# Polynomial-sketch attention into a tanh FFN: VectorE's attention written as one numbered sequence, q loaded and laid out by load, groups cut at batch 0's end

## The chip, the cores and the metric

The kernel runs on one core of a Trainium2 chip. The engines are TensorE (PE in the rows, its weight loads PEld), VectorE (DVE), ScalarE (ACT), GpSimd (POOL) and SyncE (SP), which here only issues transfers. Each engine works through its own list of instructions in order. The metric is the device time of one execution in microseconds, and less is better.

## The reference

```python
batch, n_heads, seq, head_dim = 4, 4, 1088, 32          # r = 8, d_model 128, d_ff 2048
a, b = S1 @ x, S2 @ x                                   # 8 numbers each, for every row x of q and of k
phi(x) = outer(a, b).reshape(64)
kv  = einsum('bhsf,bhsd->bhfd', phi(k), v);   z = phi(k).sum(over s)
attn = (phi(q) @ kv) / (phi(q) @ z + 1e-6)              # [4, 4, 1088, 32]
x = attn.transpose(0, 2, 1, 3).reshape(4352, 128)
h = x @ w_in;   out = (h - tanh(h)) @ w_out             # 4352 x 2048 between
```

## The kernel before, in words

**Attention of a batch.** k and q of a batch (four heads, 1088 rows) lie in 34 chunks of 32 columns and are turned by VectorE (`kT<-kL` L485, `qT<-qL` L559). TensorE makes the sketches of k (L491), which VectorE turns back (`abk<-psa`, L496). VectorE forms the outer products `w` in three pieces (L522), and TensorE sums them with v (L532). A small product `gram`, `gm`, `sc` (L505 to L515) gives the denominators. `kvd` and `kvb` bring the sum into place. The q side does the same: sketch (L570), `abq` (L575), `cq` (L586), then `m`, `den`, `rd`, `ap` (the division, L598 to L607), the outer products `qp` (L623), their transposition `qpT` (L628), and 32 products with `kvb` on TensorE (L636), each kept as two in the trace. ScalarE or VectorE copies the result into `xT`, bf16, 128 x 4352 columns. Everything of the attention on TensorE goes into four PSUM banks, `psa`. The q side works on blocks of 128 columns: batch 0 in the pieces 0 to 2, 2 to 5 and 5 to 9, the other batches in 0 to 5 and 5 to 9.

**FFN.** The columns of `xT` are cut into groups (`GCOLS`). For each group 16 products with slices of w_in (L699, "first products") go to three PSUM banks `psh`; ScalarE takes tanh of each (`th`, L702); 16 products with w_out (L712) and two with the folded weight w_in·w_out (`wch`, `wcl`, L716) add up in one bank `pso`. VectorE turns the sum (`ot`, L721), and four or eight transfers write it out. So 34 products of TensorE and 16 tanh of ScalarE go with each group. The folded weight is made at the start from casts of the weights (`wi`, `wo`), transposes (`wiT`) and 16 small products.

**What sets the order.** A planner in the program (`_Prog.schedule`) holds estimated durations, takes for each engine the operation that can start first, and among those that can start within 30 ns of it the one with the smallest key; the result is one fixed list per engine. Keys are due times: the attention of batch b is due some microseconds ahead of the group that needs it. When TensorE has nothing for over 350 ns before the first group, it gets filler products on zeros (L367). SyncE's queue issues the loads in the order of their keys.

Of the kernel before, what the change touches and what calls it, by code (L numbers as in the profile page):

```python
# [816 lines left out]
```

## Time and profile before

| | us |
|---|---|
| time, median of three runs | 131.1 (130.19 to 131.17) |
| the profiled execution, its own time | 132.3 |
| its span, first to last instruction | 130.5 |
| busy: TensorE / ScalarE / VectorE / GpSimd | 111.9 / 85.2 / 72.1 / 1.8 |

The span is what the trace covers; 1.8 us of the profiled execution lie outside it. Busy times overlap between engines and are means over stages that differ.

### The profile page before, as it was taken

Reading aid. Unit: us, or ns where it says so; the run is one execution under the profiler, and the core shown is the slowest. Engines: PE = TensorE matmul, PEld = TensorE weight load, DVE = VectorE, ACT = ScalarE, POOL = GpSimd, SP = SyncE. Lnnn points to the kernel's source line nnn. Section 1 sums busy time; section 2 is a strip of 40 time slices with the busy share of each in tenths; the row PEclk is TensorE's granted clock in tenths of the full one; section 3 lists DMA queues with packets and bytes.
Section 4 is the critical chain, followed back from the end, with each engine's and each line's share of the span. In section 5 each row is a group of like instructions: output and inputs, shape, how many; then the busy total and the mean of one; then the engine's idle time right before and its main releaser. Section 6 shows DMA issues by size and latency. Waiting matters only on the chain.

```text
span 130.5 us, 3757 instructions
## 1 busy us (share of the span) xinstructions
PE 111.9 (86%) x1602; PEld 54.7 (42%) x1618; DVE 72.1 (55%) x155; ACT 85.2 (65%) x189; POOL 1.8 (1%) x14
## 2 busy tenths in 40 slices
PE   6998989674048899899899999999999999999990
PEld 4856656341022452333543444453335433334460
DVE  5368678496934969963728982641997201002010
ACT  0315822751014269578587899659789999999990
POOL 4100000000000000000000000000000000000000
PEclk9999999999855699999999999999999999999999
DMA  2999999999700000040000410400040130401322
GB/s 43 287 312 343 337 222 319 209 306 201 166 20 0 0 8 0 5 68 17 0 0 5 65 15 18 68 5 0 0 71 14 28 57 0 70 10 25 61 39 41
DMA packets 25552, 11.28 MB, mean 86 GB/s; under 512 B 19136, under 2 KB 24000, under 8 KB 25536
## 3 DMA queue, kind: packets, MB, share of 16 engines
q1 hardware_dynamic: 24528, 10.44, 35.4%
q10 hardware_dynamic: 1008, 0.61, 1.8%
q8 instruction: 12, 0.20, 0.7%
q14 instruction: 4, 0.03, 0.1%
HBM read 8.81 MB, written 2.23 MB: 85 GB/s over the span
## 4 chain that ended last, share of the span: by engine, by line
PE 48%; SPq 12%; DVE 12%; ACT 11%; DMA 11%; issue 3%
PE pso L712 16%; PE psh L699 16%; SPq L393 12%; DMA qL<-in_q_dram 11%; ACT th L702 10%; PE psa L636 6%; PE psa L532 3%; DVE w L522 3%; PE pso L716 2%; PE psa L491 2%; DVE abk L496 2%; DVE ot L721 1%; DVE qT L559 1%; PE psa L570 1%; ACT xT L318 1%
## 5 line engine op out<-in xcount | busy, mean ns | idle before, releaser
L702 ACT ACTIVATE th<-psh 128x512 bf16<-128x512 f32 (+3 forms) x160 | 72.0, 566 | 10.2 <-PE psh L699 9.3
L699 PE MATMUL psh<-xT,wi 128*128 128x512 bf16 (+3 forms) x152 | 51.9, 353 | 2.7 <-ACT th L702 1.2
L712 PE MATMUL pso<-th,wo 128*128 128x512 bf16 (+3 forms) x154 | 49.3, 349 | 1.1 <-issue 0.5
L699 PEld LDWEIGHTS psh<-xT,wi 128*128 128x128 bf16 x160 | 15.3, 98 | 24.2 <-ACT th L702 14.7
L712 PEld LDWEIGHTS pso<-th,wo 128*128 128x128 bf16 x160 | 15.3, 98 | 19.2 <-ACT th L702 7.0
L721 DVE STREAM_TRANSPOSE ot<-pso 128x512 f32<-128x512 f32 (+3 forms) x10 | 6.3, 635 | 25.7 <-PE pso L712 25.7
L636 PE MATMUL psa<-qpT,kvb 32*32 32x128 f32 (+3 forms) x576 | 10.1, 294 | 6.8 <-DVE qpT L628 6.8
L318 ACT CAST xT<-psa 128x384 bf16<-128x384 f32 (+3 forms) x11 | 5.1, 479 | 14.5 <-PE psa L636 14.5
L367 PE MATMUL pso<-zz 128*128 128x256 bf16 x86 | 12.6, 296 | 1.1 <-DVE zz L366 1.1
L628 DVE STREAM_TRANSPOSE qpT<-qp 128x512 f32<-128x512 f32 (+1 forms) x16 | 11.5, 755 | 0.1
L623 DVE TENSOR_TENSOR qp<-ap,abq 128x512 f32<-128x512 f32 (+1 forms) x16 | 11.3, 744 | 0.2
L522 DVE TENSOR_TENSOR w<-abk 128x768 f32<-128x768 f32 x12 | 11.1, 949 | 0.1
L636 PEld LDWEIGHTS psa<-qpT,kvb 32*32 32x32 f32 x576 | 6.6, 106 | 10.4 <-DVE qpT L628 7.5
L367 PEld LDWEIGHTS pso<-zz 128*128 128x128 bf16 x86 | 8.6, 106 | 3.2 <-DVE zz L366 1.1
L496 DVE STREAM_TRANSPOSE abk<-psa 128x288 f32<-128x288 f32 x8 | 3.4, 459 | 8.1 <-PE psa L491 8.1
L559 DVE STREAM_TRANSPOSE qT<-qL 128x448 f32<-128x448 f32 (+3 forms) x9 | 6.1, 673 | 2.9 <-DMA qL<-in_q_dram 2.9
L532 PE MATMUL psa<-w,vL 128*32 128x64 f32 x288 | 6.5, 223 | 1.2 <-DVE w L522 1.2
L575 DVE STREAM_TRANSPOSE abq<-psa 128x288 f32<-128x288 f32 (+3 forms) x12 | 3.9, 359 | 6.3 <-PE psa L570 6.3
L485 DVE STREAM_TRANSPOSE kT<-kL 128x576 f32<-128x576 f32 (+1 forms) x8 | 5.6, 718 | 3.1 <-DMA kL<-in_k_dram 3.1
L532 PEld LDWEIGHTS psa<-w,vL 128*32 128x32 f32 x288 | 4.7, 110 | 4.2 <-DVE w L522 3.6
L662 ACT CAST wi<-wi_f 128x512 bf16<-128x512 f32 x4 | 2.5, 620 | 4.5 <-DMA wi_f<-in_moe_w_in_dram 4.3
L491 PE MATMUL psa<-kT,wab 64*32 64x288 f32 x64 | 3.4, 481 | 1.3 <-ACT xT L318 1.1
(54 smaller groups left out, 59.1 us busy)
## 6 DMA issues: line engine op xcount, KB each, us to landing
kL<-in_k_dram SPq DMA_DIRECT2D x3, 544.0 KB, 11.9
vL<-in_v_dram SPq DMA_DIRECT2D x9, 144.0 KB, 12.5
wi_f<-in_moe_w_in_dram SPq DMA_DIRECT2D x4, 256.0 KB, 6.2
wo_f<-in_moe_w_out_dram SPq DMA_DIRECT2D x4, 256.0 KB, 7.2
out_dram<-ot SPq DMA_DIRECT2D x16, 64.0 KB, 2.0
qL<-in_q_dram SPq DMA_DIRECT2D x3, 320.0 KB, 13.8
qL<-in_q_dram SPq DMA_DIRECT2D x4, 224.0 KB, 12.7
vL<-in_v_dram ACTq DMA_DIRECT2D x3, 144.0 KB, 3.9
```

What stands on the lines that cost most here:

```text
L367: filler = (lambda e, n: e.matmul(bank_o.slots[0][0][:, 0:256], zz.ap[:, 0:128], zz.ap[:, 128:384], start=True, stop=True), zop, bank_o)
L393: return P.add({eng: (430.0, 0.0)}, lambda e, n: e.dma_start(out=o_, in_=i_), w=w, key=key, dma=nbytes)
L522: P.add(_v(768), lambda e, n, p=p, wv=wv: e.tensor_tensor(out=wv.ap.rearrange("p (x i j) -> p x i j", i=8, j=8), in0=abh()[:, 0, p * 12:(p ...
L532: i = e.matmul(psa4[h * 32:(h + 1) * 32, 2, 0:64], vL[b][:, h, blk * 32:(blk + 1) * 32], wv.ap[:, (bi * 4 + h) * 64:(bi * 4 + h + 1) * 64] ...
L559: P.add(_v((z - a) * 32), lambda e, n, a=a, z=z: e.transpose(qT.ap[:, a * 32:z * 32], qL[b][:, a * 32:z * 32]), r=[val], w=[qT], key=max(k ...
L623: P.add(_v(cn * 256), lambda e, n, aq=aq, qp=qp, av=av, c0=c0, c1=c1, cn=cn: e.tensor_tensor(out=qp.ap[:, 0:cn * 256].rearrange("p (x i j) ...
L628: P.add(_v(cn * 256), lambda e, n, qp=qp, qt=qt, c0=c0, c1=c1, cn=cn: e.transpose(qt.ap[:, c0 * 256:c1 * 256], qp.ap[:, 0:cn * 256]), r=[q ...
L636: i = e.matmul(psa4[h * 32:(h + 1) * 32, g, 0:nb * 32], kvb.ap[g * 32:(g + 1) * 32, x, h * 32:(h + 1) * 32], qq[g * 32:(g + 1) * 32, 0:nb, ...
L699: P.add(_pe(n_ / 2.4 + 2.6), lambda e, n, jb=jb, hv=hv: e.matmul(hv.ap[:, 0:n_], wi[jb // 4].ap[:, (jb % 4) * 128:(jb % 4 + 1) * 128], xt, ...
L702: P.add(_a(n_), lambda e, n, hv=hv, th=th: e.activation(out=th.ap[:, 0:n_], in_=hv.ap[:, 0:n_], func=AF.Tanh, scale=-1.0), r=[hv], w=[th], ...
L712: fn = lambda e, n, x=x, st=st, sp_=sp_: e.matmul(ov.ap[:, 0:n_], wo[x // 4].ap[:, x % 4, :], ths[x].ap[:, 0:n_], start=st, stop=sp_)
L721: P.add(_vp(n_), lambda e, n: e.transpose(ot.ap[:, 0:n_], ov.ap[:, 0:n_]), r=[ov], w=[ot], key=-60000)
```

## The change

Attention steps are written as functions (`k_transposes`, `k_sketch`, `gram`, `k_outer`, `kv_mm`, `q_sketch`, `q_divide`, `q_piece` and others), and their keys come from one counter (`nk`), so that their order in the program is their rank; `attention_first` and `attention` call them. For VectorE the planner now picks the smallest key among all that can start within 150 ns (60 for TensorE and ScalarE) instead of 30. q's transposed layout gets a buffer for each batch, and each load its own part of it. Batch 0's q comes in two loads (8 and 26 chunks) instead of three and the others' in one instead of two; the first goes ahead of v and the weights, the second behind the first slice of w_in; v of batch 0 waits for the small load of S2. Batch 0's later q blocks (2 to 9) go through one sketch and one division, in the FFN's banks `psh` and `pso`, not `psa`. The copies `sc`, `kvd`, `kvb` and all `xT` are ScalarE's alone. One slice of w_in and two of w_out are cast by GpSimd. The groups become 256, 384, 448, six of 512, and 192; the first three end where batch 0 ends. The tanh buffers go from 28 to 24, those of `w` from 4 to 3.

```diff
-GCOLS = [256] + [512] * 7 + [384, 128]
+GCOLS = [256, 384, 448] + [512] * 6 + [192]
+WINDOW = {"tensor": 60.0, "vector": 150.0, "scalar": 60.0, "gpsimd": 30.0, "sync": 30.0}
...
-                t, o = min(((t, o) for t, o in cands if t <= t0 + 30.0), key=lambda x: (x[1].key, x[0]))
+                t, o = min(((t, o) for t, o in cands if t <= t0 + WINDOW[e]), key=lambda x: (x[1].key, x[0]))
...
-    qT_p = pool("qT", 2, [128, 36 * 32])
+    qTs = [sb("qT", [128, 36 * 32]) for _ in range(B)]
...
-    qcut = {0: [0, 8, 20, 34]}
+    qcut = {0: [0, 8, 34]}
...
+            load(key + g, vL[b][g * 32:(g + 1) * 32, :, 0:w_], vs, [vvals[b][g]], 128 * w_ * 4, eng, rate=205.0,
+                 after=[s_load] if eng == "scalar" else ())
...
     load_k(next(lk), 0)
+    load_q(next(lk), 0, 0)
     load_v(next(lk), 0, "scalar")
-    load_q(next(lk), 0, 0)
     load_wi(next(lk), 0)
...
     load_q(next(lk), 0, 1)
+    for i in range(1, 4):
+        load_wi(next(lk), i)
+    for i in range(4):
+        load_wo(next(lk), i)
...
+    def attention_first():
+        b = 0
+        k_transposes(b)
+        q_transpose(b, 0)
+        k_sketch(b)
+        gram(b)
+        k_outer(b, 0)
+        ab, cq = _Val(abq_p), _Val(cq_p)
+        ab2, cq2 = _Val(abq_p), _Val(cq_p)
+        q_sketch(b, 0, 2, ab, bk[0:2])
+        gram_tail(b)
+        k_outer(b, 1)
+        k_outer(b, 2)
+        q_gram(b, 0, 2, cq, bk[3])
+        kv_mm(b)
+        kv_tail(b)
+        aq = q_divide(b, 0, 2, ab, cq)
+        q_piece(b, 0, 0, 2, ab, aq)
+        q_transpose(b, 1)
+        hb = [_Val(bank_h), _Val(bank_o), _Val(bank_h)]
+        q_sketch(b, 2, 9, ab2, hb[0:2])
+        q_gram(b, 2, 9, cq2, hb[2])
+        aq = q_divide(b, 2, 9, ab2, cq2)
+        q_piece(b, 2, 2, 5, ab2, aq)
+        q_piece(b, 2, 5, 9, ab2, aq)
+
+    def attention(b):
+        k_transposes(b)
+        for i in range(len(qvals[b])):
+            q_transpose(b, i)
+        k_sketch(b)
+        gram(b)
+        k_outer(b, 0)
+        gram_tail(b)
+        ab, cq = _Val(abq_p), _Val(cq_p)
+        q_sketch(b, 0, 9, ab, bk[0:2])
+        k_outer(b, 1)
+        k_outer(b, 2)
+        q_gram(b, 0, 9, cq, bk[3])
+        kv_mm(b)
+        kv_tail(b)
+        aq = q_divide(b, 0, 9, ab, cq)
+        q_piece(b, 0, 0, 5, ab, aq)
+        q_piece(b, 0, 5, 9, ab, aq)
...
-            P.add(_as(512), lambda e, n, i=i: e.copy(wi[i].ap[:, :], wif[i].ap), r=[wif[i]], w=[wi[i]], key=-1000 + i)
+            P.add({**_as(512), **_g(512)}, lambda e, n, i=i: copy(e, n, wi[i].ap[:, :], wif[i].ap), r=[wif[i]], w=[wi[i]], key=-1000 + i, name=f"wi{i}")
```

How this moves instructions is shown at three places. In the names, `kL_6` to `kL_9`, `vL_10` to `vL_13` and `qL_14` to `qL_17` are the batches 0 to 3, and a number behind another name is a buffer. "waits d_sync_N" is a wait for a load.

VectorE before, from the last piece of batch 0 (blocks 5 to 9):

```order
L575 STREAM_TRANSPOSE abq_26<-psa_5 128x4x2x16
L586 STREAM_TRANSPOSE cq_29<-psa_5 128x128 [waits e_tensor]
L559 STREAM_TRANSPOSE qT_20<-qL_16 128x640 [waits d_sync_26]
L598 TENSOR_TENSOR m_40<-abq_26,cq_29 128x16x8 [waits e_vector]
L559 STREAM_TRANSPOSE qT_20<-qL_16 128x448 [waits d_sync_27]
L602 TENSOR_REDUCE den_44<-m_40 128x16 [waits e_vector]
L605 RECIPROCAL rd_46<-den_44 128x16 [waits e_vector]
L607 TENSOR_TENSOR ap_42<-abq_26,rd_46 128x128 [waits e_vector]
L623 TENSOR_TENSOR qp_36<-ap_42,abq_26 128x512 [waits e_vector]
L623 TENSOR_TENSOR qp_34<-ap_42,abq_26 128x512
L628 STREAM_TRANSPOSE qpT_39<-qp_36 128x512 [waits e_vector]
L628 STREAM_TRANSPOSE qpT_39<-qp_34 128x512 [waits e_vector]
```

Two transpositions of batch 2's q (`qL_16`), each with a wait for its load, stand between the steps of batch 0's last piece. VectorE after, from the division of batch 0's blocks 2 to 9:

```order
L633 TENSOR_TENSOR ap_44<-abq_27,rd_48 128x224 [waits e_vector]
L651 TENSOR_TENSOR qp_36<-ap_44,abq_27 128x768 [waits e_vector]
L656 STREAM_TRANSPOSE qpT_39<-qp_36 128x768 [waits e_vector]
L651 TENSOR_TENSOR qp_37<-ap_44,abq_27 128x512
L656 STREAM_TRANSPOSE qpT_40<-qp_37 128x512 [waits e_vector]
L651 TENSOR_TENSOR qp_35<-ap_44,abq_27 128x512
L656 STREAM_TRANSPOSE qpT_40<-qp_35 128x512 [waits e_vector]
L496 STREAM_TRANSPOSE kT_19<-kL_7 128x576 [waits d_sync_13]
L496 STREAM_TRANSPOSE kT_19<-kL_7 128x512
L754 TENSOR_TENSOR wcl_106<-psh_3,wch_105 128x128 [waits e_scalar]
L503 STREAM_TRANSPOSE qT_21<-qL_15 128x1088 [waits d_sync_18]
L789 STREAM_TRANSPOSE ot_81<-pso_4 128x256 [waits e_tensor]
```

Here batch 0 is done to its last `qpT` before anything of batch 1 comes, and the next wait for a load is that for batch 1's k.

ScalarE before, from `sc` of batch 0 to its first `xT`:

```order
L318 COPY sc_52<-psa_5 128x32 [waits e_tensor]
L662 CAST wi_100<-wi_f_96 128x512 [waits d_sync_6]
L318 COPY wiT_106<-psh_1 128x1024 [waits e_tensor]
L662 CAST wi_101<-wi_f_96 128x512 [waits d_sync_7]
L318 COPY kvb_54<-psa_5 128x256 [waits e_tensor]
L318 CAST wo_102<-wo_f_97 128x512 [waits d_sync_9]
L318 CAST wo_103<-wo_f_97 128x512 [waits d_sync_10]
L318 CAST wo_104<-wo_f_97 128x512 [waits d_sync_12]
L318 CAST wo_105<-wo_f_97 128x512 [waits d_sync_13]
L685 CAST wch_108<-psh_3 128x128 [waits e_tensor]
L318 CAST xT_87<-psa_5 128x256 [waits e_tensor]
```

ScalarE after, to the first tanh:

```order
L319 CAST wi_97<-wi_f_93 128x512 [waits d_sync_7]
L542 COPY sc_53<-psa_5 128x32 [waits e_tensor]
L319 COPY wiT_103<-psh_1 128x1024 [waits e_tensor]
L319 CAST wo_99<-wo_f_94 128x512 [waits d_sync_9]
L319 COPY kvd_49<-psa_5 128x256 [waits e_tensor]
L319 CAST wo_100<-wo_f_94 128x512 [waits d_sync_10]
L319 COPY wiT_104<-psh_2 128x1024 [waits e_tensor]
L319 COPY kvb_55<-psa_5 128x256 [waits e_tensor]
L319 CAST xT_84<-psa_5 128x256 [waits e_tensor]
L770 ACTIVATE th_57<-psh_2 128x256 [waits e_tensor]
```

`kvd` was on VectorE and is here; `kvb` now stands behind two casts of w_out and the second `wiT`, where it stood ahead of them; two casts of w_out and one of w_in have gone to GpSimd.

TensorE before, around the k sketch of batch 3 (L491, `kT_19`); `wi_98` is the first slice of w_in, and each slice serves four first products of a group:

```order
L712 MATMUL pso_4<-th_62,wo_105 128x512
L699 MATMUL psh_2<-xT_87,wi_98 128x512
L712 MATMUL pso_4<-th_63,wo_105 128x512
L636 MATMUL psa_5<-qpT_37,kvb_54 32x128 x32
L699 MATMUL psh_3<-xT_87,wi_99 128x512
L699 MATMUL psh_1<-xT_87,wi_99 128x512
L712 MATMUL pso_4<-th_64,wo_102 128x512
L712 MATMUL pso_4<-th_65,wo_102 128x512
L712 MATMUL pso_4<-th_66,wo_102 128x512
L491 MATMUL psa_5<-kT_19,wab_94 32x288 x8
L712 MATMUL pso_4<-th_67,wo_102 128x512
L699 MATMUL psh_2<-xT_87,wi_99 128x512
```

TensorE after, around the same sketch (L516); here `wi_95` is the first slice:

```order
L767 MATMUL psh_3<-xT_84,wi_98 128x512
L780 MATMUL pso_4<-th_68,wo_101 128x512
L665 MATMUL psa_5<-qpT_38,kvb_55 32x128 x32
L767 MATMUL psh_2<-xT_84,wi_95 128x512
L780 MATMUL pso_4<-th_69,wo_102 128x512
L767 MATMUL psh_1<-xT_84,wi_95 128x512
L780 MATMUL pso_4<-th_70,wo_102 128x512
L516 MATMUL psa_5<-kT_19,wab_91 32x288 x8
L767 MATMUL psh_3<-xT_84,wi_95 128x512
L780 MATMUL pso_4<-th_71,wo_102 128x512
L767 MATMUL psh_2<-xT_84,wi_95 128x512
L780 MATMUL pso_4<-th_72,wo_102 128x512
```

Before, the sketch comes behind six first products of the fifth group; now, behind two of the fifth. Counted in columns of first products that stand ahead of the k sketches of the batches 1, 2 and 3, these are 288, 992 and 1984 before, and 376, 1004 and 1664 after.

## Rows read from the trace of the kernel before

**Rows 1.** Windows: busy us and instructions of each engine, granted clock, DMA share, GB/s.

```profile
0.00:22.29 22.29, 19.67 (x341) 13.95 (x342) 14.55 (x36) 7.93 (x15) 1.81 (x14) 1.00 0.95 265
22.29:31.15 8.86, 6.79 (x123) 3.26 (x121) 6.62 (x16) 5.11 (x17) 0.00 (x0) 1.00 1.06 249
31.15:39.76 8.61, 1.52 (x65) 1.06 (x66) 5.08 (x12) 0.59 (x2) 0.00 (x0) 0.71 0.51 106
39.76:59.91 20.15, 18.60 (x311) 7.48 (x322) 15.27 (x31) 13.14 (x27) 0.00 (x0) 0.87 0.09 15
59.91:81.78 21.87, 20.92 (x330) 9.40 (x342) 14.35 (x30) 17.64 (x36) 0.00 (x0) 1.00 0.10 17
81.78:103.52 21.74, 20.78 (x323) 9.52 (x329) 13.71 (x28) 17.31 (x36) 0.00 (x0) 1.00 0.15 23
103.52:127.24 23.72, 23.34 (x129) 9.91 (x128) 2.24 (x4) 23.48 (x61) 0.00 (x0) 1.00 0.26 40
127.24:130.50 3.26, 0.28 (x2) 0.10 (x1) 0.32 (x1) 0.00 (x0) 0.00 (x0) 0.96 0.28 41
```

**Rows 2.** Timeline, VectorE, 20 to 40 us: start, duration, what, idle before and its releaser.

```profile
20.51 1.37 DVE L485 STREAM_TRANSPOSE kT<-kL 128x576 f32<-128x576 f32 x2 [0.55 <-DMA kL<-in_k_dram]
...
24.18 0.85 DVE L559 STREAM_TRANSPOSE qT<-qL 128x640 f32<-128x640 f32 x1 [1.02 <-DMA qL<-in_q_dram]
...
25.77 0.65 DVE L559 STREAM_TRANSPOSE qT<-qL 128x448 f32<-128x448 f32 x1 [0.64 <-DMA qL<-in_q_dram]
...
26.60 0.96 DVE L623 TENSOR_TENSOR qp<-ap,abq 128x768 f32<-128x768 f32 x1
...
31.15 0.27 DVE L586 STREAM_TRANSPOSE cq<-psa 128x128 f32<-128x128 f32 x1
32.15 0.85 DVE L559 STREAM_TRANSPOSE qT<-qL 128x640 f32<-128x640 f32 x1 [0.73 <-DMA qL<-in_q_dram]
...
34.56 1.29 DVE L623 TENSOR_TENSOR qp<-ap,abq 128x512 f32<-128x512 f32 x2
35.77 1.30 DVE L628 STREAM_TRANSPOSE qpT<-qp 128x512 f32<-128x512 f32 x2
```

**Rows 3.** Timeline, TensorE, 18 to 40 us: the products with kvb.

```profile
20.01 0.85 PE L636 MATMUL psa<-qpT,kvb 32*32 32x64 f32 x64
...
37.12 1.52 PE L636 MATMUL psa<-qpT,kvb 32*32 32x128 f32 x64 [6.16 <-DVE qpT L628]
```

**Rows 4.** Timeline, ScalarE, 8 to 60 us.

```profile
12.50 1.01 ACT L318 COPY wiT<-psh 128x1024 bf16<-128x1024 bf16 x1 [0.25 <-PE psh L670]
...
14.03 0.37 ACT L318 COPY kvb<-psa 128x256 f32<-128x256 f32 x1
14.29 1.66 ACT L318 CAST wo<-wo_f 128x512 bf16<-128x512 f32 x3
...
20.90 0.37 ACT L318 CAST xT<-psa 128x256 bf16<-128x256 f32 x1 [1.53 <-PE psa L636]
...
25.02 2.87 ACT L702 ACTIVATE th<-psh 128x256 bf16<-128x256 f32 x10 [0.96 <-PE psh L699]
...
47.84 5.60 ACT L702 ACTIVATE th<-psh 128x512 bf16<-128x512 f32 x11
```

**Rows 5.** Timeline, SyncE's queue: issue of the first two slices of w_out.

```profile
5.68 1.01 SPq L393 DMA_DIRECT2D wo_f<-in_moe_w_out_dram  x2
```

**Rows 6.** The page's part 6: issues, KB each, median us from issue to landing.

```profile
wo_f<-in_moe_w_out_dram SPq DMA_DIRECT2D x4, 256.0 KB, 7.2
```

**Rows 7.** The chain that ended last: start, us, what.

```profile
39.76 1.29 PE psa L491 x16
...
81.13 0.65 PE pso L712 x3
81.78 0.73 PE psa L491 x16
```

**Rows 8.** Groups by shape, GpSimd: busy us, mean ns of one.

```profile
L376 POOL CAST identb<-ident 128x128 bf16<-128x128 f32 x1 | 0.3, 289 | 0.0
```

More of the change, by code (lines that the diff above doesn't have):

```diff
@@ L448, in bass_polysketch_attn__then__act_tanh_shrink_kernel @@
         load_v(next(lk), b)
-        for i in range(2):
-            load_q(next(lk), b, i)
+        load_q(next(lk), b, 0)
     gstart = []
@@ new lines, in bass_polysketch_attn__then__act_tanh_shrink_kernel, with k_outer @@
+    wvs = {}
+    def k_outer(b, p):
+        ab = abk[b]
+        wv = wvs[b, p] = _Val(w_p)
+        abh = lambda x: ab.ap.rearrange("p x k (h i) -> p x (k h) i", h=4)[:, x, p * 12:(p + 1) * 12]
+        P.add(_v(768), lambda e, n: e.tensor_tensor(
+            out=wv.ap.rearrange("p (x i j) -> p x i j", i=8, j=8),
+            in0=abh(0)[:, :, :, None].to_broadcast([128, 12, 8, 8]),
+            in1=abh(1)[:, :, None, :].to_broadcast([128, 12, 8, 8]),
+            op=ALU.mult), r=[ab], w=[wv], key=nk(), name=f"w{b}.{p}")
@@ L518, in k_side, with kv_mm @@
+    def kv_mm(b):
         prev = None
         for p in range(3):
[L520 to L526 removed]
@@ L536, in kvmm, with kv_tail @@
                 return i
[L537 to L540 removed]
+            prev = P.add(_pe(3 * 2 * 56 + 30), mm, r=[wvs[b, p]] + vvals[b], w=[bk[2]], key=nk(), chain=prev,
+                         mode="128x32", name=f"kvmm{b}.{p}")
+    def kv_tail(b):
+        kvd, kvb = _Val(kvd_p), kvbv[b]
+        P.add(_a(256), lambda e, n: copy(
@@ new lines, in kv_tail, with q_in, qv4, q_sketch @@
+        P.add(_pe(240), kvt, r=[kvd, ident], w=[bk[2]], key=nk(), mode="128x128", name=f"kvt{b}")
+        P.add(_a(256), lambda e, n: copy(
+            e, n, kvb.ap.rearrange("p x c -> p (x c)"), bk[2].ap[:, 0:256]),
+            r=[bk[2]], w=[kvb], key=nk(), name=f"kvb{b}")
+    def q_in(b, s0, s1):
+        return [v_ for (a, z, v_) in qTv[b] if a < s1 * 4 and z > s0 * 4]
+    def qv4(b):
+        return qTs[b].rearrange("p (k g t) -> p k g t", g=4, t=32)
+    def q_sketch(b, s0, s1, ab, banks):
+        sn = (s1 - s0) * 32
+        def sk(e, n):
+            for g in range(4):
+                for rh in range(2):
+                    i = e.matmul(banks[rh].ap[g * 32:(g + 1) * 32, 0:sn], wab.ap[rh * 64:(rh + 1) * 64, :],
+                                 qv4(b)[rh * 64:(rh + 1) * 64, s0:s1, g, :], start=True, stop=True)
+            return i
+        P.add(_pe(sn * 4 / 2.4 + 60), sk, r=q_in(b, s0, s1) + [wab], w=list(banks), key=nk(), mode="64x32",
+              name=f"qsk{b}.{s0}")
+        back(b, banks, ab, s1 - s0, f"qab{s0}.")
@@ new lines, in q_gram, with ck @@
+    def q_gram(b, s0, s1, cq, bank):
+        sn = (s1 - s0) * 32
+        sc = scv[b]
+        def ck(e, n):
+            for g in range(4):
+                i = e.matmul(bank.ap[g * 32:(g + 1) * 32, 0:sn], sc.ap[:, :], qv4(b)[:, s0:s1, g, :],
+                             start=True, stop=True)
+            return i
+        P.add(_pe(sn * 4 / 2.4 + 30), ck, r=q_in(b, s0, s1) + [sc], w=[bank], key=nk(), mode="128x32", name=f"ck{b}.{s0}")
+        P.add(_vp(sn), lambda e, n: e.transpose(
+            cq.ap[:, 0:s1 - s0, :].rearrange("p k f -> p (k f)"), bank.ap[:, 0:sn]),
+            r=[bank], w=[cq], key=nk(), name=f"cq{b}.{s0}")
```

322 lines of the change are left out of this document (137 added, 185 removed).

## Prediction, written before the changed kernel ran

> **What bounds the kernel now.** I read the windows first, with edges at the first tanh (22.29), at the last step of batch 0 that still ran freely (31.15), at the k sketches of the batches 1, 2 and 3 (39.76, 59.91, 81.78), and at the first and last tanh of the stretch in which ScalarE never pauses (103.52, 127.24) [rows 1]. [...] To 22.29 no tanh runs: loads at 265 GB/s, and the attention of the first two blocks. [...] From 59.91 to 103.52 TensorE is the bound (20.92 of 21.87 us, 20.78 of 21.74). From 103.52 on ScalarE is (23.48 of 23.72).
>
> VectorE's timeline names the hole. Its steps for batch 0 stand behind transpositions of q of the batches 1 and 2, whose loads land at 24.18, 25.77 and 32.15 [rows 2]; the last piece of batch 0 is ready at 37.07, TensorE waited 6.16 us for it [rows 3], and only then does anything of the second group start.
>
> **The start.** The chain to the first tanh runs over ScalarE, in order. Its slowest link in the new list is the second slice of w_out, whose cast stands ahead of the second `wiT` and of `kvb`. Before, that slice was issued near 6.2 [rows 5] and landed 7.2 later [rows 6], at 13.4. Now 224 KB more of batch 0's q lie ahead of it: at 265 GB/s 0.9 us, so 14.3. Then a cast of 0.55 (three in 1.66), `wiT` 1.01, `kvb` 0.37 [rows 4]: 16.2. From the first product with `kvb` to the start of `xT` it was 0.89 (20.01 to 20.90) [rows 3, 4], and from there to the first tanh 1.39 (to 22.29) with the sketch of three blocks between. With seven blocks I add 0.4, an estimate. First tanh near 18.9, against 22.29. The other chains end sooner: v of batch 0 comes 1.5 us later, which costs nothing as long as it lands before the first `w` is done; w_in's last slice lands some 1 us ahead of w_out's first (13.8), so near 12.8, and its cast on GpSimd, four times the 128 columns that took 0.289 [rows 8], is 1.16 us, then four transposes: 14.5, where `wiT` can start at 14.85. That cover is only 0.35 us thick; a longer cast goes straight into the start.
>
> **The hole.** From the second sketch (near 17.7) VectorE has no wait for a load in front of batch 0's end. The small steps took 1.2 us for four blocks before (31.15 to 34.56, less the wait of 0.73 and the two transpositions of 0.85 and 0.65) [rows 2]; for seven blocks with the sketch's own transpositions I take 2.6. Then `qp` and its turn for three blocks, twice 0.96, and for four, 1.29 and 1.30 [rows 2]: 24.8. From the last product with `kvb` to the next k sketch it was 2.64 (37.12 to 39.76) at the low clock [rows 3, 7]; at the full one I take 2.2. So batch 1's k sketch starts at **27.1** instead of 39.76. Its k transposition (1.37) fits into these 2.2 us, and its k has long landed (20.51) [rows 2]. All bytes ahead of batch 1's q are the same as before, so it lands near 25.77 and is turned from 26.2 on: the cover is thin again, 0.4 us.
>
> **Batches 1 and 2, sketch to sketch.** A group of 512 columns costs TensorE 34 products of 0.217 us (three in 0.65) [rows 7], 7.4 us. The stretch from 59.91 to 81.78 covers 992 columns by the order, 14.3 us, which leaves 7.6 for a batch's attention and all small waits; the next has 960 columns, 13.8, and leaves 7.9. Between the k sketches of batch 1 and batch 3 now lie 1664 - 376 = 1288 columns instead of 1696: 18.5 + 2 x 7.75 = 34.0. VectorE needs, for a batch, the 14.35 busy us of that stretch [rows 1] and the transpositions of the next batch's k and q, 1.37 and about 1.5: 17.2, twice 34.4. `kvd` and `kvb` leave it, a merged division saves a few fixed costs, one more `ot` comes. So both engines are nearly full; I take **34.4**, where it was 42.02, of which the lower clock had a part. The third sketch falls at 61.5.
>
> **From there to the end.** The next 21.74 us did 960 columns and the rest of batch 3, at TensorE's pace [rows 1], and 1408 columns were then left for ScalarE, 23.72 us. Now 4352 - 1664 - 960 = 1728 are left: ten more tanh of 512 columns at 0.51 (eleven in 5.60) [rows 4], 5.1 us. The narrow groups at the end shrink from 384 and 128 to 192, which saves 0 to 1.2; I take 0.6. So 28.2, and after the last tanh 3.26 as before: **53.2**, where it was 48.72. The cut of the groups itself costs nothing else I can price: 34 products and 16 tanh for each of ten groups, 4352 columns, both times.
>
> Sum: 27.1 + 34.4 + 53.2 = 114.7 us of span. The profiled execution took 132.3 for a span of 130.5, so 1.8 more: 116.5. The median of the three runs is 131.1, 0.991 of that execution: **115.4 us**.
>
> **Unknown costs, both ends.** w_out's second slice: in the old run it had landed by 14.84 at the latest, since its cast did not wait [rows 4], so +1.4; or the q bytes do not delay it, -0.9. The two nearly full engines: VectorE's two copies gone take up to 1.7 us off the stretch of 34.4 if TensorE's residue shrinks as well; waits of one for the other add up to 2 us a batch (a third of TensorE's worst wait here, 6.16). The end: in the new order batch 3's last product with `kvb` stands behind 2272 columns, not the 2624 that I assume, and ScalarE would run freely sooner if VectorE keeps pace, -1.0. Together 111.8 to about 121.
>
> **Rivals.** (1) GpSimd and VectorE get into each other's way. The row for GpSimd is one cast of 0.289 us beside small VectorE work [rows 8]; no row shows a long cast beside VectorE's two-input products, of which one takes 0.96 [rows 2]. If each of three casts waits for one such product, or holds one up, by about 1 us, the start slips by 0.65 (behind the cover of 0.35) and VectorE's chain of batch 0 by up to 2: 115.4 + 2.7 = 118.1. [...] (2) VectorE and TensorE take turns instead of overlapping. For it: both lists are in order, VectorE has hardly a spare microsecond a batch; against: in the stretches of 21.8 TensorE was busy 20.9 although VectorE's steps had to come in time. Price 2 us for each of three batches: 121.4. (3) The change does not do what it says: VectorE's list still waits for a load. If the undivided q of batch 1 lands as late as batch 2's did (32.15), the transposition in front of `abk` ends near 33.6 instead of 28: +5.5, 120.9. Against it, its place among the bytes is unchanged. (4) Slower than before: TensorE's clock. It stood at its lower level after 6 us without work, and the k sketch's 16 parts took 1.29 us there against 0.73 [rows 7]. If the waits of batch 1 bring it down and it stays down to the third sketch, the 34.0 us of TensorE's work there become up to 68, +34, and 149; it decides from 15.7 us of loss on, that is, from nearly half of that stretch at the low level. Against it: between 59.91 and 127.24 the clock stood at 1.00 through all short waits [rows 1].
>
> **How the numbers follow.** The forecast as worked, 113 to 117: 0.58. Below it, the savings of the bounds, 110.5 to 113: 0.09. Rival 1: 0.12. Rival 2: 0.12. Rival 3: 0.05. Rival 4: 0.04. A range from 111.5 to 121 leaves out rival 4, part of the savings, and the worse halves of the rivals 2 and 3: some 0.17. About 1% is what a measurement of this kernel can tell from no change, and only rival 4 and a small remainder reach there: faster by over 1% 0.95, within 1% 0.01, slower 0.04.
>
> **What would show it.** The first tanh at 18 to 20; no wait of VectorE for q behind 20 us that exceeds 1 us; the k sketches of the batches 1 and 3 near 27 and 61.5; the clock at 1.00 from 17 us on; ScalarE without a pause in the last 28 us. A first tanh behind 21 would say that GpSimd or w_out's landing was mis-sized; a third sketch behind 65, that VectorE and TensorE take turns; a clock below 1.00 in that stretch, rival 4. The sum as a whole fails if the k sketch of batch 1 starts near 27 and the rest takes more than 92 us.

## The result, and the profile after

| | before | after |
|---|---|---|
| median, us | 131.13 (130.19 to 131.8) | 125.35 (123.08 to 126.68) |
| profiled execution, its span | 132.3, 130.5 | 123.08, 121.3 |
| first tanh | 22.29 | 22.11 (forecast 18.9) |
| k sketch of batch 1 starts | 39.76 | 31.00 (27.1), then stops; the rest from 34.20 |
| k sketch of batch 3 | 81.78 | 67.41 (61.5) |
| from there to the end | 48.72 | 53.89 (53.2) |

The ratio is 0.944, 95% interval 0.931 to 0.957: 5.6% faster, where 12% was forecast (115.4, range 111.5 to 121.0). Disturbed executions (two of the four of the changed kernel) count in the medians but not in the ratios, from which gains are read below (0.01 is 1.3 us); the profiles of the kernel before, of E2 and of E4 are of such executions.

Windows of the kernel after, with edges at the first tanh, at the k sketches of the batches 1, 2 and 3, and where the first of them goes on after its stop (columns as in [rows 1]):

```profile
0.00:14.35 14.35, 10.23 (x126) 7.32 (x127) 8.14 (x20) 3.14 (x4) 2.55 (x17) 0.93 0.81 236
14.35:22.11 7.76, 7.76 (x172) 5.29 (x170) 4.12 (x11) 4.17 (x9) 1.56 (x3) 0.68 1.10 269
22.11:31.00 8.89, 8.40 (x181) 4.70 (x180) 8.62 (x16) 7.28 (x24) 0.00 (x0) 1.00 1.05 277
31.00:34.20 3.20, 0.67 (x3) 0.13 (x3) 0.43 (x1) 0.72 (x2) 0.00 (x0) 1.00 1.06 235
34.20:50.95 16.75, 16.54 (x313) 8.39 (x313) 15.36 (x26) 11.52 (x29) 0.00 (x0) 1.00 0.18 34
50.95:67.41 16.46, 15.73 (x305) 7.73 (x308) 15.35 (x26) 12.71 (x28) 0.00 (x0) 1.00 0.10 16
67.41:121.30 53.89, 49.47 (x461) 19.00 (x466) 16.90 (x28) 45.54 (x102) 0.00 (x0) 1.00 0.21 33
```

Three things stand out. From 34.20 on each stretch is within 1.2 us of its forecast, and up to 67.41 TensorE is nearly full (16.54 of 16.75 us in the first of the two windows) with VectorE close behind (15.36). But the start has gained nothing, at a granted clock of 0.68, and 3.2 us vanish in the middle of one sketch, at a clock of 1.00, with the engines nearly idle and the DMA full. TensorE's timeline names the two waits (start, duration, what, idle before and its releaser):

```profile
10.52 0.34 PE L599 MATMUL psa<-qT,wab 64*32 64x64 f32 x16
12.88 0.87 PE L563 MATMUL psa<-w,vL 128*32 128x64 f32 x24 [2.02 <-DMA vL<-in_v_dram]
...
31.00 0.67 PE L516 MATMUL psa<-kT,wab 64*32 64x288 f32 x3
34.20 0.71 PE L516 MATMUL psa<-kT,wab 64*32 64x288 f32 x13 [2.54 <-issue]
```

The first is v of batch 0, which came too late and left TensorE idle for 2.02 us; its granted clock is 0.50 from 12.5 to 19.2, and 1.00 on both sides of that. The second is "issue": three of the sketch's sixteen products run and thirteen do not, although all their operands are there and they are one loop of the code. Something that no semaphore shows was missing. The page's part 3 lists a DMA queue of the kind "instruction" (`q8`); its 12 transfers are 16 KB each, and one of them moves at 31.5, inside the stop:

```profile
q1 hardware_dynamic: 23760, 10.43, 37.5%
q10 hardware_dynamic: 1136, 0.62, 1.9%
q8 instruction: 12, 0.20, 0.7%
```

**Theory F**, formed on this: TensorE's instructions come in blocks through the same DMA engines as the loads, and this block came late, behind data. **Theory V**: the start was lost to v's late landing. The rivals stand with each run.

### The profile page after: what moved, and what is told of

The parts are those of the page before. It is cut to its first block, busy times and chain, and to the rows that moved or that the text cites. A ratio compares the mean times of both kernels' runs of the same rounds, so it can differ in the third digit from the quotient of the medians.

```text
span 121.3 us, 3619 instructions
## 1 busy us (share of the span) xinstructions
PE 108.8 (90%) x1553; PEld 52.6 (43%) x1563; DVE 68.9 (57%) x124; ACT 85.1 (70%) x194; POOL 4.1 (3%) x19
## 4 chain that ended last, share of the span: by engine, by line
PE 75%; DMA 9%; ACT 5%; issue 4%; DVE 3%; ACTq 1%
PE pso L780 24%; PE psh L767 24%; PE psa L665 8%; DMA vL<-in_v_dram 7%; PE psa L563 5%; ACT th L770 4%; DVE ot L789 2%; PE pso L784 2%; PE psa L516 2%; DMA sin<-in_S_dram 2%; PE pso L368 2%; PE psa L599 2%; PE psa L612 2%; PE psa L540 1%; PE psh L738 1%
## 5 line engine op out<-in xcount | busy, mean ns | idle before, releaser
L770 ACT ACTIVATE th<-psh 128x512 bf16<-128x512 f32 (+4 forms) x160 | 71.5, 579 | 11.7 <-PE psh L767 9.9
L767 PE MATMUL psh<-xT,wi 128*128 128x512 bf16 (+4 forms) x157 | 53.6, 351 | 1.6 <-issue 0.3
L780 PE MATMUL pso<-th,wo 128*128 128x512 bf16 (+4 forms) x156 | 48.6, 347 | 1.0 <-issue 0.8
L789 DVE STREAM_TRANSPOSE ot<-pso 128x512 f32<-128x512 f32 (+4 forms) x10 | 6.3, 635 | 37.0 <-PE pso L780 29.3
L656 DVE STREAM_TRANSPOSE qpT<-qp 128x512 f32<-128x512 f32 (+1 forms) x16 | 12.4, 776 | 0.5
L368 PE MATMUL pso<-zz 128*128 128x256 bf16 x55 | 9.6, 346 | 1.1 <-DVE zz L367 1.1
L563 PE MATMUL psa<-w,vL 128*32 128x64 f32 x288 | 7.4, 245 | 2.0 <-DMA vL<-in_v_dram 2.0
L368 PEld LDWEIGHTS pso<-zz 128*128 128x128 bf16 x55 | 6.7, 125 | 3.5 <-DVE zz L367 1.1
L563 PEld LDWEIGHTS psa<-w,vL 128*32 128x32 f32 x288 | 5.6, 123 | 5.1 <-DVE w L550 4.0
L503 DVE STREAM_TRANSPOSE qT<-qL 128x1088 f32<-128x1088 f32 (+2 forms) x5 | 5.3, 1058 | 1.3 <-DMA qL<-in_q_dram 1.3
L516 PE MATMUL psa<-kT,wab 64*32 64x288 f32 x64 | 3.5, 415 | 2.7 <-issue 2.5
```

The lines of the kernel that those rows point to most:

```text
L368: filler = (lambda e, n: e.matmul(bank_o.slots[0][0][:, 0:256], zz.ap[:, 0:128], zz.ap[:, 128:384], start=True, stop=True), zop, bank_o)
L516: i = e.matmul(bk[rh].ap[g * 32:(g + 1) * 32, 0:288], wab.ap[rh * 64:(rh + 1) * 64, :], kT[b].ap[rh * 64:(rh + 1) * 64, g * 288:(g + 1) * ...
L563: i = e.matmul(bk[2].ap[h * 32:(h + 1) * 32, 0:64], vL[b][:, h, blk * 32:(blk + 1) * 32], wvs[b, p].ap[:, (bi * 4 + h) * 64:(bi * 4 + h + ...
L656: P.add(_v(cn * 256), lambda e, n, qp=qp, o0=o0, cn=cn: e.transpose(qt.ap[:, o0 * 256:(o0 + cn) * 256], qp.ap[:, 0:cn * 256]), r=[qp], w=[ ...
L767: P.add(_pe(n_ / 2.4 + 2.6), lambda e, n, jb=jb, hv=hv: e.matmul(hv.ap[:, 0:n_], wi[jb // 4].ap[:, (jb % 4) * 128:(jb % 4 + 1) * 128], xt, ...
L770: P.add(_a(n_), lambda e, n, hv=hv, th=th: e.activation(out=th.ap[:, 0:n_], in_=hv.ap[:, 0:n_], func=AF.Tanh, scale=-1.0), r=[hv], w=[th], ...
```

## The experiments

Twelve kernels. The helper `at(engine, name)` finds an operation in an engine's finished order; edits behind the scheduler leave every other order as it is.

| run | median, us | ratio to before, 95% | first tanh | k sketch of batch 1 | TensorE's stops of 0.5 us and more, by issue |
|---|---|---|---|---|---|
| after | 125.35 | 0.944 (0.931 to 0.957) | 22.11 | 31.00 | 2.54 |
| E1 v first | 123.25 | 0.937 (0.930 to 0.945) | 20.17 | 30.32 | 1.20, 1.25, 2.42 |
| E2 hold part of batch 3 | 122.35 | 0.931 (0.925 to 0.938) | 21.83 | 32.25 | 1.52, 1.60 |
| E3 idle products | 126.91 | 0.968 (0.957 to 0.978) | 21.79 | 36.09 | 0.78, 4.14 |
| E4 the three | 122.12 | 0.929 (0.921 to 0.936) | 20.80 | 32.40 | 0.82, 1.40 |
| E5 hold batches 2, 3 | 118.82 | 0.908 (0.905 to 0.912) | 21.25 | 29.97 | none |
| E6 E5 and v first | 117.74 | 0.899 (0.894 to 0.903) | 20.17 | 28.89 | 1.07 |
| E7 groups of before | 126.94 | 0.966 (0.957 to 0.974) | 20.80 | 31.09 | 1.16, 2.95 |
| E8 before, VectorE's order | 130.44 | 0.995 (0.992 to 0.998) | 23.00 | 37.35 | none |
| E9 E6, batch 1 held too | 117.89 | 0.903 (0.893 to 0.912) | 19.88 | 28.60 | 0.58 |
| E10 E9, q behind w_in | 117.66 | 0.898 (0.891 to 0.906) | 19.30 | 28.02 | none |
| E11 two sketches | 121.45 | 0.928 (0.919 to 0.936) | 20.80 | 35.15 | 1.21 |
| E12 no casts on GpSimd | 117.90 | 0.901 (0.894 to 0.908) | 20.01 | 28.73 | 1.20 |

**E1, v first.** Behind the scheduler:

```diff
+    for o in P.order["scalar"]:
+        if o.dma:
+            o.deps.pop(s_load, None)
```

> The four loads of batch 0's v no longer wait for the load of S2 on ScalarE's queue; everything else is as in the changed kernel. Theory V (v came too late): they are issued near 1.4 instead of 2.9, v lands near 9.5 instead of 12.9, the first product of w and v no longer waits 2.0 us, TensorE's clock stays at 1.00 to 20 us, and the first tanh starts 2 to 3 us sooner (19 to 20 instead of 22.1): 121 to 123.5 us. Rival W (the weights set the start): v is sooner but the casts of w_in still end at 13.6 and the last product chain on ScalarE is as late; first tanh within 0.7 us of 22.1, time within 1%. Rival L (shared bandwidth): k and q of batch 0 land later by what v takes, first tanh unchanged or later, 124 to 127.

V holds for the start: the first product of w and v goes at 11.32, the clock stays at 1.00 to 33 us, and the first tanh comes 1.94 us sooner. But the k sketch of batch 1 goes on at 33.41 instead of 34.20: TensorE now stops three times, and the ratios, 0.937 and 0.944, cannot be told apart. Its timeline, and windows between the stops:

```profile
18.16 0.71 PE L665 MATMUL psa<-qpT,kvb 32*32 32x64 f32 x48 [1.20 <-issue]
...
26.00 0.70 PE L665 MATMUL psa<-qpT,kvb 32*32 32x96 f32 x36 [1.25 <-issue]
...
33.41 1.18 PE L516 MATMUL psa<-kT,wab 64*32 64x288 f32 x13 [2.42 <-issue]
```

```profile
18.10:25.95 7.85, 6.25 (x128) 2.89 (x128) 6.20 (x12) 5.01 (x17) 0.00 (x0) 1.00 1.07 268
25.95:33.35 7.40, 4.84 (x128) 3.00 (x127) 3.61 (x6) 3.37 (x9) 0.00 (x0) 1.00 1.02 258
```

From stop to stop TensorE ran 128 products and 128 or 127 weight loads, whatever their kind. The page of the changed kernel has 12 transfers of 16 KB in `q8` for 1553 products and 1563 weight loads, some 260 instructions each; so I read one transfer, a block below, as 128 products with their weight loads. With the DMA full (shares of 1.07 and 1.02) one came in 7.85 and in 7.40 us. That supply is what TensorE ran at here, and the sooner start only met it sooner.

**E2, part of batch 3 held.**

```diff
+    hold = P.order["tensor"][at("tensor", "ksk1")]
+    P.order["sync"][27].deps[hold] = False
```

> The loads of batch 3 wait until the k sketch of batch 1 is done; the order on each engine is that of the changed kernel. Theory F (TensorE stands at 31 us because its next block of instructions comes late, behind data loads): with 1.6 MB less under way the loads end near 25, the block lands in time, the stop of 2.5 us inside the k sketch goes, and the time falls by 2 to 3.5 us (121 to 123). Rival S (the stop belongs to this place in the program, for instance to the sketch's operands or its bank): it stays at 2.5 us, time within 1%. Rival H (batch 3 now comes too late): its loads land near 40, long before its k is turned near 60, so nothing is lost; a loss would show as a wait for k behind 60.

The edit held less than I wrote: the 27th entry is batch 3's second load of v, so 0.94 MB waited, not 1.6. The stop in the sketch fell from 2.54 to 1.60, with another of 1.52 ahead of it. By the ratios the time is 1.7 us shorter, but their intervals overlap. So E2 fits F and does not prove it. The stop that stayed looks odd, since the DMA share is 0.05 from 33 to 34 us. But the loads end near 31, not near 25 as expected (the share is 0.99 from 29 to 30), and the block begins to move at 32.20, behind them; TensorE goes on 2.32 later. In all sixteen stops of the table TensorE goes on 2.3 to 3.1 us after a block has begun to move. What fills that time is not shown.

**E3, idle products.** 19 more fillers, meant to keep TensorE's clock up:

```diff
+    warm("kvmm0.0", 16)
+    warm("kvmm0.1", 3)
```

> Sixteen idle products of 256 columns more on TensorE ahead of the first product of w and v, three more ahead of the second; v still comes late. Theory C (the low clock, not the wait itself, costs the start): the clock stays at 1.00 from 10 to 21 us, the steps between 12.9 and 21.8 shorten, first tanh near 20 to 20.8, time 122.5 to 124. Rival D (the wait itself is the loss, the chain runs over VectorE and ScalarE at their own pace): clock 1.00 but first tanh at 21.5 to 22.3, time within 1%. The stop inside the k sketch of batch 1 should move to 19 products earlier in the program if it belongs to a block of instructions, and stay in the sketch if it belongs to the sketch.

On the start inconclusive: the clock fell to 0.50 while the sixteen ran (2.99 us), so the product of w and v went at 14.00, and the higher clock behind it gave back what they had cost (21.79). On the stop it is plain:

```profile
29.82 0.95 PE L665 MATMUL psa<-qpT,kvb 32*32 32x128 f32 x51
34.92 0.44 PE L665 MATMUL psa<-qpT,kvb 32*32 32x128 f32 x13 [4.14 <-issue]
36.09 1.21 PE L516 MATMUL psa<-kT,wab 64*32 64x288 f32 x16
```

Thirteen of these products are left, then three of group 1 follow, then the three of the sketch that ran before: the stop stands 19 products earlier, and the sketch runs whole. It belongs to an instruction's number, not to the sketch (rival S falls), and an idle product was not free: it used up the block. The time is 3.1 us longer by the ratios.

The count goes further than 19. Windows from the start into the stops of E1, and into the long stops of the changed kernel and of E3:

```profile
0.00:17.50 17.50, 14.19 (x221) 9.84 (x222) 11.66 (x28) 6.82 (x11) 4.46 (x19) 1.00 0.92 260
0.00:25.30 25.30, 20.43 (x349) 12.73 (x350) 17.21 (x39) 11.83 (x28) 4.46 (x19) 1.00 0.96 262
0.00:32.50 32.50, 25.28 (x477) 15.72 (x477) 21.47 (x45) 15.20 (x37) 4.46 (x19) 1.00 0.98 261
0.00:33.00 33.00, 27.06 (x477) 17.44 (x477) 21.31 (x45) 15.31 (x37) 4.12 (x19) 0.90 0.96 255
0.00:33.00 33.00, 26.74 (x477) 17.63 (x478) 21.32 (x45) 13.84 (x33) 4.30 (x19) 0.95 0.96 248
```

All sixteen stops of the table stand behind TensorE's product 221, 349 or 477, each 128 further on, whatever product comes next: with 19 idle products more (E3), with two more (E12), with other groups (E7). That is the strongest sign that the stops belong to blocks of instructions.

**E4, the three together**, the edits as above.

> The three edits together. If V and F hold and add: 118 to 121 us, first tanh near 19 to 20, no stop of TensorE over 1 us between the first tanh and the end. If the start is set by the weights and only F holds: 121 to 123. If neither: within 1% of the changed kernel.

122.12, in the range of the second case, though the first tanh, at 20.80, is sooner than in the changed kernel. By the ratios E1 gained 0.8 us, E2 1.7, E3 lost 3.1, and the three together gain 2.0: the edits do not simply add, but the intervals are about 2 us wide, so that E4 decides nothing.

**E5, batches 2 and 3 held.**

```diff
+    P.order["sync"][19].deps[P.order["tensor"][at("tensor", "ksk1")]] = False
```

> All loads of the batches 2 and 3 wait until the k sketch of batch 1 is done; nothing else differs from the changed kernel. Theory F (TensorE's instruction blocks queue behind data loads): about 5.6 MB are left ahead of that sketch, so the data ends near 22; every later block lands within 4 us, no stop of TensorE put down to issue exceeds 0.6 us between 24 and 36, the sketch ends near 30.5 instead of 34.9, and the time falls by 3 to 4.5 us (121 to 122.5). Rival R (the fetch is slow by itself, some 8 us a block whatever the data does): stops as before, within 1%. Rival H (batch 2 comes too late): VectorE waits for k or q of batch 2 near 42, and the time is as much longer.

One line, and the time is 4.6 us shorter by the ratios (0.908 and 0.944, intervals well apart); 118.82 lies below the range expected. The profiled span is 4.2 shorter. Windows, edges as above:

```profile
14.35:21.25 6.90, 6.77 (x171) 4.44 (x169) 4.23 (x11) 4.06 (x9) 1.86 (x3) 0.85 1.10 283
21.25:29.97 8.72, 8.23 (x180) 4.68 (x179) 8.45 (x16) 7.28 (x24) 0.00 (x0) 1.00 0.08 27
29.97:46.73 16.76, 16.55 (x316) 8.40 (x316) 15.95 (x27) 12.25 (x31) 0.00 (x0) 1.00 0.88 222
46.73:63.19 16.46, 16.26 (x309) 7.74 (x308) 15.36 (x26) 12.71 (x28) 0.00 (x0) 1.00 0.11 17
63.19:117.10 53.91, 50.25 (x467) 19.01 (x466) 16.91 (x28) 45.54 (x102) 0.00 (x0) 1.00 0.21 33
```

Set beside the windows of the changed kernel, each later stretch is the same to 0.2 us; only the 3.20 are gone, and 0.9 of the start, where the clock came back near 16.4 us instead of 19 (nothing shows that the edit did this). With the DMA share at 0.08 the blocks move at 21.65 and 26.43, 4.8 us apart, and nothing stops: F holds, R falls. The held loads come with a share of 0.88 later and cost nothing there: H falls too. Why no stop comes in that window is not shown: TensorE runs 316 products in its 16.76 us, 128 in 6.8 us, hardly slower than in the stretch before (180 in 8.72, 128 in 6.2).

**E6, E5 with v first**, batch 3 held until the k sketch of batch 2.

> As the one before, with batch 3 held until the k sketch of batch 2 and batch 0's v not waiting for S2. Theory F: with the supply of instructions out of the way the sooner start counts: first tanh 19 to 20.2, k sketch of batch 1 whole by 28, 117 to 119.5 us. If the start is bound by TensorE's supply of instructions even then (the first blocks still come beside loads): first tanh near 20.2 to 20.8 with one stop of about 1 us left ahead of it, 118.5 to 120.5. If F falls: 122 to 124, as with v alone.

117.74. The sooner start now counts: 1.08 us at the k sketch, as at the first tanh, and 1.3 us by the ratios, with intervals apart. One stop of 1.07 is left, inside the first product with `kvb`: that is the expectation's second case, while the first tanh (20.17) and the time are in the ranges of its first; the sketch, at 28.89, is later than its 28.

**E7, the groups of before** in the changed kernel.

```diff
-GCOLS = [256, 384, 448] + [512] * 6 + [192]
+GCOLS = [256] + [512] * 7 + [384, 128]
```

> The cut of the columns into groups as before the change (256, seven of 512, 384, 128); the rest is the changed kernel. My prediction had the cut at nothing but 0.6 us for narrower last groups: then 125 to 127. Theory G (the cut is part of the gain): the second group now needs the third piece of batch 0, ScalarE stands until that is there, first tanh of the second group 2 us later, and it counts: 126.5 to 129. Theory F: the wide groups spend fewer instructions ahead of the k sketch of batch 1, so the stop there comes later in the program, and some of this loss is given back.

126.94, in the ranges of both cases; by the ratios 2.9 us slower, with intervals that just touch. The second group's first tanh comes at 31.20 instead of 28.32, as G says, but the k sketch of batch 1 comes 10.29 behind the first tanh, about as in E1 (10.15), whose groups are those of the change and whose start is nearly as soon. From the k sketch of batch 3 (67.73) to the end it is 55.67 instead of 53.89: the cut is worth some 1.8 us at the end. One thing more: this run has the start of the changed kernel, v at 12.53 and a wait of 1.64 for it, and yet its first tanh comes at 20.80, since the clock was back at 1.00 from 16 us on instead of 19.

**E8, VectorE's order in the kernel before.**

```diff
+    for names, behind in ((("qT1",), "qpT0"), (("kT2", "qT2"), "w1")):
+        mv = [o for p in names for o in pick(p)]
+        last = pick(behind)[-1]
+        lst[:] = [o for o in lst if o not in mv]
+        i = lst.index(last) + 1
+        lst[i:i] = mv
...
```

> The kernel before, with six of VectorE's instructions in another place: the transpositions of q of batch 1 behind the last piece of batch 0, those of k and q of batch 2 behind the last w of batch 1. Loads, groups and start are those of before. Theory O (the hole was VectorE's order, and filling it is nearly the whole gain): the k sketch of batch 1 moves from 39.8 to 33 to 35, the clock stays up, 123.5 to 126.5. Rival P (the order alone does little, the loads and the groups of the change are needed with it): 128 to 131.

A miss, and P is right: 0.5%, 0.6 us. Behind 20 us VectorE waits for a load only once, 0.39 us, yet the k sketch starts at 37.35, 14.35 us behind the first tanh, where it was 17.47 in a profile of 132.3 us, 1.2 above the median. VectorE and TensorE instead (two timelines):

```profile
25.33 0.98 DVE L628 STREAM_TRANSPOSE qpT<-qp 128x768 f32<-128x768 f32 x1
29.48 0.45 DVE L721 STREAM_TRANSPOSE ot<-pso 128x256 f32<-128x256 f32 x1 [3.16 <-PE pso L712]
30.13 0.52 DVE L575 STREAM_TRANSPOSE abq<-psa 128x128 f32<-128x128 f32 x2 [0.21 <-PE psa L570]
```

```profile
28.05 0.96 PE L636 MATMUL psa<-qpT,kvb 32*32 32x96 f32 x64
...
29.58 0.45 PE L570 MATMUL psa<-qT,wab 64*32 64x128 f32 x16
...
34.72 1.52 PE L636 MATMUL psa<-qpT,kvb 32*32 32x128 f32 x64 [4.33 <-DVE qpT L628]
```

The sketch of the last four blocks uses the same banks as the products of the three before it; it waits for them, they stand behind group 0 in TensorE's list, and only then does VectorE's chain of small steps begin again.

**E9 and E10, the rest of the start.** E9 holds batch 1's loads until the first product with `kvb`; E10 also issues the second load of q behind w_in:

```diff
+    P.order["sync"][13].deps[P.order["tensor"][at("tensor", "num0.0")]] = False
```
```diff
+    lst = P.order["sync"]
+    lst.insert(8, lst.pop(5))
...
```

> As the kernel with v early and the batches 2 and 3 held (117.74 us), and batch 1's loads too wait, until the first product with kvb is done. Theory F: the last stop of TensorE ahead of the first tanh (1.07 us inside that product) is the third block of instructions behind data; with fewer bytes queued at 11 to 15 us the block comes sooner, the stop goes, first tanh near 19.1 instead of 20.2, and the time is 116.5 to 117. Rival H: batch 1's k and q land near 26 to 27 and VectorE waits for them ahead of its k sketch: the sketch starts 0.5 to 2 us later than 28.9, 117.5 to 119.5.

> As the one before, and the second load of batch 0's q (416 KB) is issued behind the four slices of w_in instead of behind the first. The chain that ended last goes through w_in's last slices (landed 12.3). Theory W (the start is now set by w_in): they land 1 to 1.5 us sooner, first tanh 0.7 to 1.3 us sooner than in the run before, 115.3 to 116.5 us. Rival Q: that q is turned just behind the first piece and now lands too late for the sketch of seven blocks; same first tanh, second piece later, 117 to 118. If instructions bound the start: no change.

In the profiles each does what F and W say: the last stop shrinks to 0.58 and goes, the first tanh moves to 19.88 and 19.30, the k sketch to 28.60 and 28.02. The times, 117.89 and 117.66, lie in the ranges of the rivals H and Q, whose waits the profiles do not have: from the first tanh to the k sketch it is 8.72 in both, as in E6. They cannot be told from E6's: what the profiles gain, 0.3 and 0.7 us of span, is below what these runs measure.

**E11, two sketches**, through the attention's banks, on E6's start, with the batches 2 and 3 held as in E5 and VectorE's transpositions of batch 2 kept behind batch 1's last piece:

```diff
-        q_sketch(b, 2, 9, ab2, hb[0:2])
-        q_gram(b, 2, 9, cq2, hb[2])
-        aq = q_divide(b, 2, 9, ab2, cq2)
-        q_piece(b, 2, 2, 5, ab2, aq)
-        q_piece(b, 2, 5, 9, ab2, aq)
+        for s0, s1 in ((2, 5), (5, 9)):
+            ab2, cq2 = _Val(abq_p), _Val(cq_p)
+            q_sketch(b, s0, s1, ab2, bk[0:2])
+            q_gram(b, s0, s1, cq2, bk[3])
+            aq = q_divide(b, s0, s1, ab2, cq2)
+            q_piece(b, s0, s0, s1, ab2, aq)
...
```

> The changed kernel with v early and the batches 2 and 3 held until the k sketch of batch 1, but the seven blocks of batch 0 go in two sketches (three blocks, four blocks) through the banks of the attention, as before the change; the transpositions of k and q of batch 2 are kept behind batch 1's last piece. Theory M (the merged sketch closes most of the hole, since the second sketch had to wait for the first one's products and copies): k sketch of batch 1 at 32 to 34.5 instead of 28.9, 121 to 124 us. Rival O (VectorE's order is what closed it; merging saves only fixed costs): 29.5 to 30.5, 118 to 119.5.

The time is in M's range, 3.7 us above E6's, and the sketch, at 35.15, is later even than M says. But the wait that M names does not show. From the first tanh to the k sketch it is 14.35 us against 8.72 with the merged sketch, E11 first:

```profile
20.80:35.15 14.35, 13.30 (x223) 6.54 (x222) 10.97 (x25) 11.77 (x35) 0.00 (x0) 1.00 0.09 29
20.17:28.89 8.72, 8.23 (x180) 4.67 (x179) 8.45 (x16) 7.28 (x24) 0.00 (x0) 1.00 0.14 42
```

TensorE is nearly full in both. With two sketches the planner puts 43 products more ahead of the k sketch, and part of that comes back: from the sketch of batch 3 (69.98) to the end (120.2) it is 50.2 instead of 53.9. So the 3.7 us are the price of two sketches, their banks and the order laid out for them together; no run parts the three.

**E12, no casts on GpSimd**, on E6.

```diff
-            P.add({**_as(512), **_g(512)}, lambda e, n, i=i: copy(e, n, wi[i].ap[:, :], wif[i].ap), r=[wif[i]], w=[wi[i]], key=-1000 + i, name=f"wi{i}")
+            P.add(_as(512), lambda e, n, i=i: copy(e, n, wi[i].ap[:, :], wif[i].ap), r=[wif[i]], w=[wi[i]], key=-1000 + i, name=f"wi{i}")
```

(and the same for w_out)

> As the kernel with v early and the batches 2 and 3 held (117.74 us), but all eight casts of weights are ScalarE's; two idle products more on TensorE. Rival 1 of the prediction (GpSimd's casts and VectorE's products hold each other up, 2 us and more on VectorE's chain): 1 to 2.5 us faster, 115.5 to 117. My present reading (a cast beside a product is late by 0.3 us at most and VectorE does not slow down): one cast more stands ahead of kvb and two ahead of xT on ScalarE, 0.55 to 0.62 each, so first tanh 0.6 to 1.8 later, 118 to 119.5.

Neither: 117.90 against 117.74. The casts moved into ScalarE's wait for TensorE's stop, so they cost nothing there, and taking them from GpSimd gave nothing. The two idle products more moved the stop two products ahead in the program, as F wants: 14 of the 64 ran before it instead of 16.

## Why the prediction was wrong

The sign was right, by a mechanism half of which was wrong; the size failed in two steps. Against the forecast span of 114.7 the profiled 121.3 is 6.6 more.

**"The start"** (18.9, measured 22.11: +3.2). The sentence that failed is that v "comes 1.5 us later, which costs nothing as long as it lands before the first `w` is done". The first `w` is done at 10.42, v is there at 12.88; its load took 6.9 us where it had taken 3.9. TensorE stood 2.02 us, its clock fell to 0.50, and the steps from 14.35 to 22.11 ran at a mean of 0.68. The sign that I had set, a first tanh behind 21, pointed at GpSimd or w_out; it was v. E1, with v early, is 1.94 sooner; most of the remaining 1.27 is the block of instructions (1.20 in E1), and E10, without a stop, comes to 19.30. How much v's lateness cost went with how long the clock then stayed down: with the same start, and the clock back at 19.2, the first tanh came at 22.11, at 21.25 in E5 (back at 16.4) and at 20.80 in E7 (back at 16). The surest figure for v is the 1.08 between E5 and E6.

**"The hole"** (from 31.15 in [rows 1] to the k sketch; 27.1, then the sketch at once). From the first tanh to the sketch I forecast 8.2 (the terms as written add up to 0.1 less) and it was 8.89. What I did not price at all is the supply of instructions: 2.54 us of stop, 3.20 of span, and, as E1 shows, it would have eaten the gain of the start as well. My "against" in every rival looked at semaphores and at the clock; the stop has neither. The shape was in the rows of before, where TensorE ran 341 products to 22.29 under full loads [rows 1]: there product 477, behind which the changed kernel stops, stands inside the hole (near 37 us), and the profile has no stop by issue beside it. The change took away the cover, with 55 idle products instead of 86 and the hole filled.

That VectorE's list made the hole was **right in part**: freeing it alone took 3.1 us from the 17.47 and 0.6 from the time (E8). The other 5.5 on the way to 8.89 came with the rest of the change; E11 does not part the merge from its banks and its order. I counted the merge as a saving of small steps and gave the gain to the list, so that this term came out near by luck.

**"Batches 1 and 2"** (34.4). Size 1.2 too high: 33.21, from 34.20 to 67.41. The mis-sized term is VectorE's 17.2 us a batch, which measured 15.36 and 15.35; TensorE set the pace (16.54 of 16.75), near the 34.0 worked out for it. The two do not take turns: rival 2 falls. Its sign, a third sketch behind 65, was there (67.41), but the time was lost ahead of 34.20.

**"From there to the end"** (53.2). 53.89, with ScalarE in the place forecast. The cut of the groups, taken at 0.6, measured some 1.8 (E7).

**Rivals.** Rival 3: no; VectorE's longest wait for q is 1.25 us, at 7.8, and none behind 20. Rival 4: the clock did fall, to 0.50 from 12.5 to 19.2, ahead of the first tanh, and stood at 1.00 from 22.11 on. The rival doubles 34.0 us to 68; the half that it takes is the 0.50 of the kernel before, from 34.7 to 44.9, where the clock stood at 1.00 to 34 and from 45 to 127. Rival 1: something of it shows, the price does not. In E6 a cast that began beside two `w` took twice as long as the next one, 1.23 us against 0.62, and the small product behind them ended 0.07 behind it (GpSimd, then VectorE):

```profile
13.05 1.23 POOL L319 CAST wi<-wi_f 128x512 bf16<-128x512 f32 x1 [9.11 <-DMA wi_f<-in_moe_w_in_dram]
15.74 0.62 POOL L319 CAST wo<-wo_f 128x512 bf16<-128x512 f32 x1 [1.45 <-DMA wo_f<-in_moe_w_out_dram]
```

```profile
12.00 1.81 DVE L550 TENSOR_TENSOR w<-abk 128x768 f32<-128x768 f32 x2
14.00 0.35 DVE L625 TENSOR_TENSOR m<-abq,cq 128x64 f32<-128x64 f32 x1
```

The `w` end at 13.81, the cast at 14.28, 0.47 later, near the 0.62 that the next one took; `m` took 0.35 where it takes 0.22 in the changed kernel. So the cast took 0.6 us more and `m` 0.13, and E12 finds nothing of it in the time. In E10 the cast began first (11.21, 0.61 us), and the two `w` beside it took 2.13 instead of 1.81.

With both failed steps mended (E6) the span is 116.0, and the sum reads 20.17 + 8.72 + 33.22 + 53.89, against the 18.9 + 8.2 + 34.4 + 53.2 of the forecast.

Open: whether a block waits in the DMA engines or at the memory behind them, what fills the 2.3 to 3.1 us between its first movement and TensorE's going on, why the held loads of E5 bring no stop when they come, and which of merge, banks and order closed the rest of the hole.

## What to carry to other kernels

Loads that are issued long before they are needed are not always free: here they delayed TensorE's own instructions, and TensorE, which ran many small products in that time, stopped for 2.54 us without a semaphore to show for it. Look for "issue" on the busiest engine inside one loop, count its instructions between such stops, and hold back the loads that have time; here one wait on the load queue was worth 4.6 us by the ratios, where the whole change had brought 7.4. And test the cause of a hole alone before giving it the gain: freeing the list that visibly waited shortened the hole by 3.1 of some 8.6 us, and the time by 0.6.

## What the runs showed of the hardware

In the changed kernel the queue of the kind "instruction" moved 12 transfers of 16 KB for 1553 products and 1563 weight loads of TensorE; in E1 TensorE ran 128 products with 128 or 127 weight loads from stop to stop, and the sixteen stops of the table stand behind product 221, 349 or 477. While loads filled the DMA (shares of 1.02 to 1.07) a block came every 7.4 to 7.9 us (E1); with the loads held (0.08) two moved 4.8 us apart and nothing stopped (E5). After a block began to move, TensorE went on 2.3 to 3.1 us later, 2.7 in the changed kernel (31.5 to 34.20). The f32 products of a k sketch counted twice: the loop of eight (L516) shows as sixteen. Idle products were paid from the same blocks: with nineteen more the kernel was 3.1 us slower by the ratios, with 2.4 us more of stops in the profile (E3).
